# Second products of 512-token slots with the tokens as moving columns, and their results scattered in quarter rows

## Chip, cores and metric

One core of one Trainium2 chip runs the whole kernel as one launch. The metric is device time in microseconds (us), here 2265.47 us, the median of 3 runs (2264.88 to 2266.15). TensorE (PE) multiplies, VectorE (DVE) and ScalarE (ACT) do elementwise work, GpSimd (POOL) issues the indirect DMAs and SyncE (SP) the other DMAs.

## What is computed

An attention with squared ReLU, and on its result a mixture of eight experts, one expert per token (N = 19968 tokens):

```
attn = np.maximum(z @ z.T / S, 0.0) ** 2          # 8 batches, S = 2496
x    = (u * (attn @ v)).reshape(N, 256)
e    = argmax(x @ w_gate)                          # one of 8 experts per token
h    = np.maximum(x[e] @ w1[e], 0.0)               # 256 -> 1024, the first product
y    = h @ w2[e]                                   # 1024 -> 256, the second product
out  = gate_w * sigmoid(x @ w_output_gate)[e] * y
```

Every float32 factor is split into a high and a low part, and a product is three matrix products (low x high, high x low, high x high).

## The kernel before

**Stage one** walks the 8 batches in chunks of up to 512 query tokens (`weigh`, L280). The steps of a `Tail` object, one per call of `advance`, then gate a chunk's result, choose each token's expert and scatter the chunk's token rows into a DRAM table `xs`, sorted by expert (L455: 16 indirect DMAs of 128 pieces for a chunk of 512). A row of `xs` is four segments of 66 words: 64 words of x, then the token's factor and its number.

**Stage two** walks slots of sorted rows. A slot is 512 tokens ("wide", 32 of them) or 256 ("narrow", 18 that always run), all of one expert. `run` takes them one after the other, and while slot i is computed it loads and prepares the next two:

- `load_x` (L655) loads a slot's rows into `sx` with four DMAs of 32 partitions, and the factor and token number of each row into `meta` with a fifth. `load_w` loads the eight weight tiles.
- `turn` (L705) transposes `sx` in 32x32 blocks, so that the features lie on the partitions; `split_x` (L715, L716) and `split_w` (L698 on ACT, L699 on DVE) make high and low parts.
- `up` is the first product: eight banks (one bank is one PSUM tile `sc` of 512 columns; there are three such tiles), each of six matmuls with the weights stationary and 512 tokens moving (L739). After each bank ACT writes the high part `hh` (L748) and DVE the low part `hl` (L749), which frees `sc`.
- `down` is the second product: per 128 tokens 24 matmuls with the hidden values of these tokens stationary and 256 weight columns moving (L767). ACT multiplies by the factor (L775) and POOL scatters 128 rows of 1 KB to `out` (L776).

After each bank of `up` and each quarter of `down` a call of `then` takes one step off the list `later` (the last chunk's `Tail`, the tables of slots) and one off `steps` (parts of the preparation of the next slot). These calls set the written order of the instructions on PE, ACT and DVE, and every engine runs its own list in that order.

`sx`, `hh`, `hl` and stage one's tiles share one pool `act` of 13 tiles of 128 x 1024 words. A new tile waits until everything that reads the one before it in that place is done:

```
y = ys[:, q]
nc.scalar.activation(out=y, in_=yp[:, :D], func=AF.Copy, scale=self.m[:, q, 0:1])
it = nc.gpsimd.indirect_dma_start(
```

Of the kernel before, what the change touches and what calls it, by code (L numbers as in the profile page):

```python
# [7 lines left out]
F32 = mybir.dt.float32  # L8
# [9 lines left out]
P = 128  # L18
# [32 lines left out]
def attention_moe(ctx, tc, zt, zq_in, ut, v, wg, w12, out):  # L51
# [14 lines left out]
    xs_rows = xs.rearrange("(n a) y -> n (a y)", a=4)  # L66

# [547 lines left out]
    def pads():  # L615
# [3 lines left out]
        nc.gpsimd.memset(pad.bitcast(I32)[:, :, SEG - 1 : SEG], NOTOK)  # L619
# [25 lines left out]
    class Slot:  # L645
        def __init__(self, g):
            self.g = g
            self.part = next(p for p in range(3) if g < sum(LENGTHS[: p + 1]))
            self.i = g - sum(LENGTHS[: self.part])
            self.n = TW if self.part < 2 else T  # L650
            self.w = [None] * 8
# [4 lines left out]
        def load_x(self):  # L656
# [4 lines left out]
            self.x = pool.tile([P, 2 * CH], F32, name="sx", tag="act", bufs=13)  # L661
            self.m = pool.tile([P, 4, 2], F32, name="meta", bufs=4)
            its = []
            for a in range(4):
                its.append(
                    nc.sync.dma_start(
                        out=self.x[a * 32 : (a + 1) * 32, 0 : 2 * n].rearrange("r (n y) -> r n y", y=64),
                        in_=rows[:, a * SEG : a * SEG + D // 4].rearrange("(n r) y -> r n y", r=32),
                    )
                )  # L670
            its.append(
                nc.sync.dma_start(
                    out=self.m[:, 0 : n // P], in_=rows[:, SEG - 2 : SEG].rearrange("(q p) d -> p q d", p=P)
                )
            )
# [26 lines left out]
        def turn(self):  # L702
# [4 lines left out]
                in_=self.x[:, 0 : 2 * n].rearrange("p (n k s) -> p k n s", k=2, s=32),  # L707
# [46 lines left out]
        def down(self, then):  # L754
            wb = self.w
            ys = pool.tile([P, 4, D], F32, name="y", tag="xr", bufs=2)
            for q in range(self.n // P):
# [17 lines left out]
                nc.scalar.activation(out=y, in_=yp[:, :D], func=AF.Copy, scale=self.m[:, q, 0:1])  # L775
# [10 lines left out]
                then()  # L786

# [51 lines left out]
    with tc.manual_schedule(engines=all_engines):  # L839
        for k in range(-4, 0):  # L840
            prepare(k, 0 if k < -2 else LEAD)
            if k < -LOOK:
                continue
            make(k + LOOK)
        for k, (b, c, jp) in enumerate(units):
            pos = k % NPAIR
            make(k + LOOK)
            if (b, c, pos) == (B - 1, NCH - 1, 8):
                slots[0].turn()
                slots[0].split_x()  # L850
            if pos == 0:
                o = [ps_o.tile([P, CH], F32, name="o") for _ in range(2)]
                nxt = Tail(b, c, o)
            weigh(b, c, jp, attn.pop(k), o, pos == 0, pos == NPAIR - 1)
            for it in tails:
                it.advance()
            if pos == 6:
                nxt.load()
            if b == B - 1:
                if (c, pos) == (1, 1):  # L860
                    table_steps = full_table(0)
                if (c, pos) >= (1, 1):
                    next(table_steps, None)
                if c == NCH - 1 and pos in (1, 3):
                    slots[0].load_w(range(2 * pos - 2, 2 * pos + 2))
                if c == NCH - 1 and 5 <= pos:
                    slots[1].load_w({5: (0, 1, 2), 6: (3,), 7: (4, 5), 8: (6,), 9: (7,)}[pos])
                if c == NCH - 1 and pos in (5, 9):
                    slots[pos // 9].load_x()
                if c == NCH - 1 and 7 <= pos <= 8:  # L870
                    slots[0].split_w(range(2 * pos - 14, 2 * pos - 12))
# [49 lines left out]
    with tc.manual_schedule(engines=all_engines):  # L921
        run(slots[: NSLOT - N_EXTRA])
# [60 lines left out]
```

## Time and profile before

| | before |
|---|---|
| median of 3 runs | 2265.47 us |
| the profiled execution | 2267.7 us |
| its span (first to last instruction) | 2265.8 us |
| PE busy | 2244.4 us (99%) |
| DVE, ACT, POOL busy | 1744.4, 1472.5, 925.8 us |
| granted TensorE clock | 0.997 of 2.4 GHz |

The profile is of one execution. Its span is 1.9 us less than the execution's own time, which is 2.2 us above the median of the other three runs. Stage one ends at about 1318 us of the span, the wide slots at 2062.5, the narrow ones with the span. Matmuls are pipelined: a matmul's recorded duration is longer than the distance to the next, so a pitch is read from start to start.

### The profile page before, as it was taken

The page shows a single profiled execution, that of the slowest core. Times are in us where ns is not written, and L with a number is a line of the kernel's source. Part 1 is how long each engine was busy: PE and PEld are TensorE (multiplying, and loading weights), DVE is VectorE, ACT ScalarE, POOL GpSimd, SP SyncE. Part 2 cuts the span into 40 slices and gives each one's busy share as a digit, 9 for nine tenths or more (in the row PEclk, how much of TensorE's full clock was granted, in tenths as well). Part 3 has the DMA queues.
Part 4 walks back from the last instruction along what each step waited for, and adds up shares of the span by engine and source line. Part 5 has one row for each costly group of instructions (what it writes and reads, how often), then busy time and mean ns, then how long its engine had stood idle before and what let it go on. Part 6 is the DMA issues. An engine that isn't in the chain of part 4 may idle for free.

```text
span 2265.8 us, 38207 instructions
## 1 busy us (share of the span) xinstructions
PE 2244.4 (99%) x12306; PEld 1965.8 (87%) x12306; DVE 1744.4 (77%) x2840; ACT 1472.5 (65%) x2311; POOL 925.8 (41%) x810
## 2 busy tenths in 40 slices
PE   9999999999999999999999989999999999999998
PEld 7888888888888888888888878999999999999998
DVE  8898889889989889889889767555555555566775
ACT  8767767767677777777677644555555555455665
POOL 0265466566565665565566654111111111111111
PEclk9999999999999999999999999999999999999999
DMA  6794785776866966966956872322331324444431
GB/s 203 185 217 164 203 194 182 211 167 206 216 159 200 223 157 199 232 160 195 230 155 183 188 178 87 96 70 66 81 92 41 92 80 130 141 122 150 117 82 62
DMA packets 406333, 346.41 MB, mean 153 GB/s; under 512 B 141293, under 2 KB 327662, under 8 KB 406128
## 3 DMA queue, kind: packets, MB, share of 16 engines
q1 hardware_dynamic: 378288, 302.34, 50.7%
q0 software_dynamic: 27840, 41.59, 6.0%
q8 instruction: 98, 1.61, 0.3%
q14 instruction: 107, 0.88, 0.1%
HBM read 272.55 MB, written 128.90 MB: 177 GB/s over the span
## 4 chain that ended last, share of the span: by engine, by line
PE 53%; issue 33%; POOL 8%; DVE 2%; DMA 2%; ACT 1%; POOLq 0%; SPq 0%; DVEq 0%; ACTq 0%
PE o L280 43%; POOL out L776 7%; PE sc L206 4%; PE sc L207 4%; PE mp L331 1%; POOL xs L455 1%; DMA z<-td 1%; DVE al L217 1%; DMA sx<-xs 0%; DMA xs<-xr,idx 0%; POOLq L776 0%; DVE t L229 0%; DMA raw<-in_w 0%; DVE t L232 0%; ACT a L208 0%
## 5 line engine op out<-in xcount | busy, mean ns | idle before, releaser
L455 POOL DMA_INDIRECT xs<-xr,idx x624 | 762.3, 1222 | 614.9 <-DVE idx L451 425.6
L280 PE MATMUL o<-ah,v 128*128 128x512 f32 (+1 forms) x3200 | 968.4, 386 | 0.9 <-DVE v L178 0.7
L280 PEld LDWEIGHTS o<-ah,v 128*128 128x128 f32 x3200 | 599.0, 188 | 109.9 <-DVE v L178 2.2
L280 PE MATMUL o<-al,v 128*128 128x512 f32 (+1 forms) x1520 | 586.1, 386 | 0.6 <-DVE al L217 0.4
L767 PE MATMUL o<-w,hh 128*128 128x256 f32 x2624 | 480.4, 283 | 0.0
L776 POOL DMA_INDIRECT out<-y,meta x164 | 160.6, 980 | 717.3 <-ACT y L775 705.9
L699 DVE TENSOR_TENSOR w<-raw,w 128x512 fp32r<-128x512 f32 x400 | 268.8, 684 | 188.8 <-ACT w L698 188.8
L767 PEld LDWEIGHTS o<-w,hh 128*128 128x128 f32 x2624 | 412.7, 192 | 1.3
L739 PE MATMUL sc<-xh,w 128*128 128x512 f32 (+1 forms) x1600 | 378.8, 353 | 7.3 <-ACT xh L715 2.6
L767 PE MATMUL o<-w,hl 128*128 128x256 f32 x1312 | 371.7, 283 | 0.5 <-DVE hl L749 0.5
L208 ACT ACTIVATE a<-sc 128x512 f32<-128x512 f32 (+1 forms) x480 | 251.3, 576 | 178.6 <-PE sc L207 177.8
L217 DVE TENSOR_TENSOR al<-a,ah 128x1024 fp32r<-128x1024 f32 (+1 forms) x232 | 274.2, 1182 | 90.2 <-ACT ah L213 83.3
L280 PEld LDWEIGHTS o<-al,v 128*128 128x128 f32 x1520 | 285.8, 188 | 56.2 <-DVE al L217 3.2
L739 PEld LDWEIGHTS sc<-xh,w 128*128 128x128 f32 x1600 | 271.8, 190 | 47.9 <-DVE hl L749 4.3
L748 ACT ACTIVATE hh<-sc 128x512 fp32r<-128x512 f32 x328 | 196.6, 600 | 129.4 <-PE sc L739 129.2
L775 ACT ACTIVATE y<-o,meta 128x256 f32<-128x256 f32 x164 | 78.0, 475 | 294.5 <-PE o L767 253.9
L767 PEld LDWEIGHTS o<-w,hl 128*128 128x128 f32 x1312 | 251.7, 192 | 2.4 <-DVE hl L749 1.1
L211 ACT ACTIVATE a<-a 128x1024 f32<-128x1024 f32 (+1 forms) x240 | 246.3, 1026 | 7.6
L749 DVE SCALAR_TENSOR_TENSOR hl<-sc,hh 128x512 fp32r<-128x512 f32 x328 | 224.0, 683 | 34.6 <-ACT hh L748 24.3
L698 ACT CAST w<-raw 128x512 fp32r<-128x512 f32 x400 | 239.9, 614 | 0.0
L739 PE MATMUL sc<-xl,w 128*128 128x512 f32 (+1 forms) x800 | 217.0, 353 | 0.5 <-DVE xl L716 0.5
L206 PE MATMUL sc<-z,hl 128*128 128x512 f32 (+1 forms) x480 | 184.0, 383 | 3.0 <-ACT a L208 1.8
(128 smaller groups left out, 2274.4 us busy)
## 6 DMA issues: line engine op xcount, KB each, us to landing
raw<-in_w SPq DMA_DIRECT2D x400, 256.0 KB
td<-t SPq DMA_DIRECT2D x160, 512.0 KB
z<-td SPq DMA_DIRECT2D x640, 128.0 KB
raw<-in_v SPq DMA_DIRECT2D x72, 256.0 KB
u<-in_ut SPq DMA_DIRECT2D x32, 512.0 KB
sx<-xs SPq DMA_DIRECT2D x128, 128.0 KB
raw<-in_zt SPq DMA_DIRECT2D x40, 256.0 KB
raw<-in_zq SPq DMA_DIRECT2D x39, 256.0 KB
```

The lines of the kernel that those rows point to most:

```text
L206: nc.tensor.matmul(out=sc[:, :w], lhsT=st, rhs=ll[:, :w], start=True, stop=False)
L208: nc.scalar.activation(out=a[:, q, :w], in_=sc[:, :w], func=AF.Relu)
L211: nc.scalar.activation(out=a[:, :, :w], in_=a[:, :, :w], func=AF.Square)
L217: nc.vector.tensor_tensor(out=al[:, :, :w], in0=a[:, :, :w], in1=ah[:, :, :w].bitcast(F32), op=ALU.subtract)
L280: nc.tensor.matmul(out=o[d][:, :w], lhsT=vv[:, q, dd], rhs=rhs, start=begins and q == 0 and k == 0, stop=ends and q == 1 and k == len(term ...
L455: it = nc.gpsimd.indirect_dma_start(out=xs[:, :], out_offset=bass.IndirectOffsetOnAxis(ap=idx[:, n : n + 1], axis=0), in_=self.xr[:, n, :] ...
L698: nc.scalar.copy(out=ww[:, 0], in_=wr)
L699: nc.vector.tensor_tensor(out=ww[:, 1], in0=wr, in1=ww[:, 0].bitcast(F32), op=ALU.subtract)
L739: nc.tensor.matmul(out=hp[:, at : at + n], lhsT=wb[2 * d + f // 4][:, ww, fs], rhs=xx[:, d, :], start=k == 0, stop=k == 5,)
L749: nc.vector.scalar_tensor_tensor(out=lo, in0=hp, scalar=0.0, in1=ho.bitcast(F32), op0=ALU.max, op1=ALU.subtract)
L767: nc.tensor.matmul(out=yp[:, :D], lhsT=hx[:, ts], rhs=wb[4 + f // 2][:, ww, ds_], start=k == 0, stop=k == 23,)
L776: it = nc.gpsimd.indirect_dma_start(out=out[:, :], out_offset=bass.IndirectOffsetOnAxis(ap=self.m.bitcast(I32)[:, q, 1:2], axis=0), in_=y, ...
```

## The change

The second product of 29 of the 32 wide slots (all but the first three) swaps its operands: the weights are stationary and 512 tokens move. It makes two halves of 24 matmuls in place of four quarters of 24. Its result has features on the partitions, so DVE transposes each half in 32x32 blocks out of PSUM into `y`, multiplies `y` by the factors, and POOL scatters it in 16 indirect DMAs of 128 quarter rows (256 bytes each) to four places per row of `out`. For this `load_x` reads the whole segment of 66 words, so that factor and token number come with each quarter, and the `meta` DMA falls away for these slots; `turn` also copies the factors (`fac`, ACT) and makes the indices (`to`, DVE). All results `y`, of the other slots too, now come out of the pool `act`. The first entry of `later` is dropped, and both stages stand in one block of fixed order. On the host the columns of w2 are permuted.

```
@@ Slot.__init__
+            self.by_rows = self.n == T or g < 3
@@ load_x
-            self.x = pool.tile([P, 2 * CH], F32, name="sx", tag="act", bufs=13)
-            self.m = pool.tile([P, 4, 2], F32, name="meta", bufs=4)
+            self.x = pool.tile([P, NB, SEG], F32, name="sx", tag="act", bufs=13)
...
-                        in_=rows[:, a * SEG : a * SEG + D // 4].rearrange("(n r) y -> r n y", r=32),
+                        in_=rows[:, a * SEG : (a + 1) * SEG].rearrange("(n r) y -> r n y", r=32),
...
+            if self.by_rows:
+                self.m = pool.tile([P, 4, 2], F32, name="meta", bufs=4)
...
@@ turn
+            if self.by_rows:
+                return
+
+            self.f = pool.tile([P, NB], F32, name="fac", bufs=3)
+            nc.scalar.copy(out=self.f[:, 0 : n // 32], in_=self.x[:, 0 : n // 32, SEG - 2])
+            self.at = pool.tile([P, NB], I32, name="to", bufs=3)
+            nc.vector.scalar_tensor_tensor(
+                out=self.at[:, 0 : n // 32],
+                in0=self.x.bitcast(I32)[:, 0 : n // 32, SEG - 1],
+                scalar=4.0,
+                in1=quarter[:, 0 : n // 32],
+                op0=ALU.mult,
+                op1=ALU.add,
             )
@@ down, now down_rows, and for 29 slots down_columns
-            ys = pool.tile([P, 4, D], F32, name="y", tag="xr", bufs=2)
+            ys = act_f("y").rearrange("p a b -> p (a b)").rearrange("p (q d) -> p q d", d=D)
...
+        def down_columns(self, then):
+            wb, n = self.w, self.n
+            nb = n // 32
+
+            y = act_f("y").rearrange("p a b -> p (a b)").rearrange("p (n y) -> p n y", y=D // 4)[:, 0:nb]
+            for half in range(2):
+                yp = ps_o.tile([P, CH], F32, name="o")
+                k = 0
+                for f in range(8):
+                    bank, at = self.hidden(f)
+                    ds_ = slice((f % 2) * D + half * P, (f % 2) * D + (half + 1) * P)
+                    hh, hl = self.h[bank]
+                    for hx, ww in ((hh, 1), (hl, 0), (hh, 0)):
+                        nc.tensor.matmul(
+                            out=yp[:, 0:n],
+                            lhsT=wb[4 + f // 2][:, ww, ds_],
+                            rhs=hx[:, at : at + n],
+                            start=k == 0,
+                            stop=k == 23,
+                        )
+                        k += 1
+                then()
+                then()
+                nc.vector.transpose(
+                    out=y[:, :, half * 32 : (half + 1) * 32], in_=yp[:, 0:n].rearrange("p (n r) -> p n r", r=32)
+                )
+            nc.vector.tensor_tensor(
+                out=y, in0=y, in1=self.f[:, 0:nb].unsqueeze(2).to_broadcast([P, nb, D // 4]), op=ALU.mult
+            )
+            for q in range(nb):
+                it = nc.gpsimd.indirect_dma_start(
+                    out=out_quarters[:, :],
+                    out_offset=bass.IndirectOffsetOnAxis(ap=self.at[:, q : q + 1], axis=0),
+                    in_=y[:, q, :],
...
@@ after stage one
-    later = [tails[0].advance] + [idle, tail.advance] * TAIL + [idle] * 8 + [pads]
+    later = [idle, tail.advance] * TAIL + [idle] * 8 + [pads]
```

DVE in the middle of the wide slots, before, from the end of one slot's first product to the second bank of the next (`w<-raw` is L699, `hl<-sc,hh` L749, `xl<-xf,xh` L716):

```order
L749 SCALAR_TENSOR_TENSOR hl<-sc,hh 128x512 x2
L716 TENSOR_TENSOR xl<-xf,xh 128x1024
L699 TENSOR_TENSOR w<-raw_15467,w 128x512
L699 TENSOR_TENSOR w<-raw_15503,w 128x512
L699 TENSOR_TENSOR w<-raw_15580,w 128x512
L749 SCALAR_TENSOR_TENSOR hl<-sc,hh 128x512
```

The same stretch of DVE in the changed kernel, where L841 is the transpose of a half, L844 the multiplication by the factors, L704 the weight split and L768 the low part, now with the semaphores that an instruction waits for (DMASW are those of POOL's DMAs):

```order
L768 SCALAR_TENSOR_TENSOR hl<-sc,hh 128x512 [waits Activation_49] x2
L735 TENSOR_TENSOR xl<-xf,xh 128x1024 [waits Activation_49]
L704 TENSOR_TENSOR w<-raw_15467,w 128x512 [waits DMAHW1_49,Activation_49]
L841 STREAM_TRANSPOSE y<-o 128x16x32 [waits PE_49]
L704 TENSOR_TENSOR w<-raw_15503,w 128x512 [waits DMAHW2_49,Activation_49]
L704 TENSOR_TENSOR w<-raw_15580,w 128x512 [waits DMAHW3_49,Activation_49]
L841 STREAM_TRANSPOSE y<-o 128x16x32 [waits PE_49]
L844 TENSOR_TENSOR y<-y,fac 128x1024 [waits DVE_49]
L768 SCALAR_TENSOR_TENSOR hl<-sc,hh 128x512 [waits DMASW4_49,DMASW3_49,DMASW5_49,DMASW2_49,DMASW6_49,DMASW1_49,DMASW7_49,DMASW0_49,Activation_49]
```

The two transposes and the multiplication stand ahead of the next slot's first low part. That low part (the last row) has a new wait for the eight semaphores of POOL's DMAs. In the built program it is for the count of the sixteenth scatter of the wide slot two before, whose `y` had the tile of the pool `act` that this `hl` takes.

PE at the end of a wide slot, before:

```order
L767 MATMUL o<-w,hh 128x256 x2
L767 MATMUL o<-w,hl 128x256
L767 MATMUL o<-w,hh 128x256
L739 MATMUL sc<-xh,w 128x512 x2
L739 MATMUL sc<-xl,w 128x512 x2
```

PE at the same place in the changed kernel (L831 is the second product, L758 the first):

```order
L831 MATMUL o<-hh,w 128x512 x2
L831 MATMUL o<-hl,w 128x512
L831 MATMUL o<-hh,w 128x512
L758 MATMUL sc<-xh,w 128x512 x2
L758 MATMUL sc<-xl,w 128x512 x2
```

Between the first products of two wide slots stand 48 matmuls of 512 columns where 96 of 256 stood.

DVE at the start of slot 0, before (`u<-o,u` is the first step of the last chunk's `Tail`):

```order
L310 SCALAR_TENSOR_TENSOR u<-o,u 128x512 x2
L699 TENSOR_TENSOR w<-raw_15328,w 128x512
L699 TENSOR_TENSOR w<-raw_15390,w 128x512
L749 SCALAR_TENSOR_TENSOR hl<-sc,hh 128x512
L699 TENSOR_TENSOR w<-raw_15330,w 128x512
```

The same place in the changed kernel:

```order
L704 TENSOR_TENSOR w<-raw_15328,w 128x512
L704 TENSOR_TENSOR w<-raw_15390,w 128x512
L768 SCALAR_TENSOR_TENSOR hl<-sc,hh 128x512
L312 SCALAR_TENSOR_TENSOR u<-o,u 128x512 x2
L704 TENSOR_TENSOR w<-raw_15330,w 128x512
```

Each step of the last chunk's `Tail` stands one call of `then` later.

## Rows read from the trace of the kernel before

**Rows 1.** Page, part 1: busy time, share of the span and instructions of each engine.

```profile
PE 2244.4 (99%) x12306; PEld 1965.8 (87%) x12306; DVE 1744.4 (77%) x2840; ACT 1472.5 (65%) x2311; POOL 925.8 (41%) x810
```

**Rows 2.** Windows: one slot: busy us (count) of PE, PEld, DVE, ACT, POOL; PE clock, DMA.

```profile
1512.90:1535.30 22.40, 22.40 (x146) 20.51 (x145) 12.77 (x18) 11.69 (x21) 3.90 (x4) 1.00 0.42 118
```

**Rows 3.** Timeline, PE: start us, us, instruction, around the end of a wide slot.

```profile
1501.40 0.28 PE L767 MATMUL o<-w,hh 128*128 128x256 f32 x1
...
1512.80 0.28 PE L767 MATMUL o<-w,hh 128*128 128x256 f32 x1
1512.91 0.63 PE L739 MATMUL sc<-xh,w 128*128 128x512 f32 x2
...
1523.82 0.28 PE L767 MATMUL o<-w,hh 128*128 128x256 f32 x1
```

**Rows 4.** Timeline, all engines: the hand-overs at the start of that slot.

```profile
1513.12 0.48 ACT L775 ACTIVATE y<-o,meta 128x256 f32<-128x256 f32 x1 [1.90 <-PE o L767]
...
1513.87 0.98 POOL L776 DMA_INDIRECT out<-y,meta  x1 [1.91 <-ACT y L775]
...
1514.50 0.60 ACT L748 ACTIVATE hh<-sc 128x512 fp32r<-128x512 f32 x1 [0.40 <-PE sc L739]
...
1515.13 0.69 DVE L749 SCALAR_TENSOR_TENSOR hl<-sc,hh 128x512 fp32r<-128x512 f32 x1 [0.31 <-ACT hh L748]
```

**Rows 5.** Groups by line, DVE, wide slots (count, busy us, mean ns, idle before).

```profile
L699 DVE TENSOR_TENSOR w<-raw,w 128x512 fp32r<-128x512 f32 x214 | 146.5, 684 | 150.1 <-ACT w L698 150.1
...
L716 DVE TENSOR_TENSOR xl<-xf,xh 128x1024 fp32r<-128x1024 f32 x26 | 31.9, 1226 | 77.8 <-ACT xh L715 77.8
```

**Rows 6.** Line L340: DVE's transpose of 512 columns out of PSUM (ns min/median/max).

```profile
L340 DVE STREAM_TRANSPOSE lt<-mp x40: 586/704/711, 64.8 to 1341.7; 128x512 f32<-128x512 f32 x32, 128x448 f32<-128x448 f32 x8
```

**Rows 7.** Timeline, POOL: the last chunk's 16 scatters, during slots 0 and 1.

```profile
1368.02 0.97 POOL L455 DMA_INDIRECT xs<-xr,idx  x1 [12.12 <-DVE idx L451]
1369.30 0.97 POOL L455 DMA_INDIRECT xs<-xr,idx  x1 [0.30 <-issue]
1370.57 1.93 POOL L455 DMA_INDIRECT xs<-xr,idx  x1 [0.30 <-issue]
1372.81 0.97 POOL L455 DMA_INDIRECT xs<-xr,idx  x1 [0.30 <-issue]
...
1380.48 1.24 POOL L455 DMA_INDIRECT xs<-xr,idx  x1 [0.30 <-issue]
...
1389.94 0.97 POOL L776 DMA_INDIRECT out<-y,meta  x1 [0.30 <-issue]
```

**Rows 8.** Timeline, DVE, beside these scatters.

```profile
1370.43 1.23 DVE L716 TENSOR_TENSOR xl<-xf,xh 128x1024 fp32r<-128x1024 f32 x1 [2.09 <-ACT xh L715]
1372.83 0.71 DVE L699 TENSOR_TENSOR w<-raw,w 128x512 fp32r<-128x512 f32 x1 [1.17 <-ACT w L698]
...
1380.19 0.68 DVE L699 TENSOR_TENSOR w<-raw,w 128x512 fp32r<-128x512 f32 x1
```

**Rows 9.** Groups by line, POOL, whole span.

```profile
L455 POOL DMA_INDIRECT xs<-xr,idx x624 | 762.3, 1222 | 614.9 <-DVE idx L451 425.6 <-issue 173.9 <-DMA sx<-xs 10.2
```

**Rows 10.** Line L455, whole span: time from issue to landing of a scatter.

```profile
L455 POOL DMA_INDIRECT xs<-xr,idx x624: 969/1088/2036, 84.0 to 1388.7; - x156
...
DMA to landing us min/median/max: 2.2/4.4/8.6
```

**Rows 11.** Line L455, 1360 to 1400 us: the same for the last chunk.

```profile
DMA to landing us min/median/max: 2.2/2.2/2.2
```

**Rows 12.** Line L776, wide slots: durations of a scatter of 1 KB rows, and landing.

```profile
L776 POOL DMA_INDIRECT out<-y,meta x107: 972/974/982, 1460.4 to 2049.1; - x107
...
DMA to landing us min/median/max: 2.4/2.4/2.9
```

**Rows 13.** Waits of PE, 1300 to 1450 us: total us, times, longest.

```profile
PE sc L739 <- DVE hl L749: 2.6, 2, 1.6
```

More of the change, by code (lines that the diff above doesn't have):

```diff
@@ L66, in attention_moe @@
     xs_rows = xs.rearrange("(n a) y -> n (a y)", a=4)
+    out_quarters = out.rearrange("n (a y) -> (n a) y", a=4)
     ones = const.tile([P, P], BF16, name="ones")
@@ L754, in down, with down_rows @@
         def down(self, then):
+            if self.by_rows:
+                self.down_rows(then)
+            else:
+                self.down_columns(then)
+        def down_rows(self, then):
             wb = self.w
-            ys = pool.tile([P, 4, D], F32, name="y", tag="xr", bufs=2)
+            ys = act_f("y").rearrange("p a b -> p (a b)").rearrange("p (q d) -> p q d", d=D)
             for q in range(self.n // P):
@@ L838, in attention_moe @@
     all_engines = {mybir.EngineType.PE, mybir.EngineType.Activation, mybir.EngineType.DVE}
[L839 to L871, printed above, removed]
-            if pos == NPAIR - 1:
-                tail = nxt
-                tails = [it for it in tails if it.step < TAIL] + [tail]
-            prepare(k)
@@ new lines, in attention_moe @@
+    ordered = ExitStack()
+    ordered.enter_context(tc.manual_schedule(engines=all_engines))
+    for k in range(-4, 0):
+        prepare(k, 0 if k < -2 else LEAD)
+        if k < -LOOK:
+            continue
+        make(k + LOOK)
+    for k, (b, c, jp) in enumerate(units):
+        pos = k % NPAIR
+        make(k + LOOK)
+        if (b, c, pos) == (B - 1, NCH - 1, 8):
+            slots[0].turn()
+            slots[0].split_x()
+        if pos == 0:
+            o = [ps_o.tile([P, CH], F32, name="o") for _ in range(2)]
+            nxt = Tail(b, c, o)
+        weigh(b, c, jp, attn.pop(k), o, pos == 0, pos == NPAIR - 1)
+        for it in tails:
+            it.advance()
+        if pos == 6:
+            nxt.load()
+        if b == B - 1:
+            if (c, pos) == (1, 1):
+                table_steps = full_table(0)
+            if (c, pos) >= (1, 1):
+                next(table_steps, None)
+            if c == NCH - 1 and pos in (1, 3):
+                slots[0].load_w(range(2 * pos - 2, 2 * pos + 2))
+            if c == NCH - 1 and 5 <= pos:
+                slots[1].load_w({5: (0, 1, 2), 6: (3,), 7: (4, 5), 8: (6,), 9: (7,)}[pos])
+            if c == NCH - 1 and pos in (5, 9):
+                slots[pos // 9].load_x()
+            if c == NCH - 1 and 7 <= pos <= 8:
+                slots[0].split_w(range(2 * pos - 14, 2 * pos - 12))
+        if pos == NPAIR - 1:
+            tail = nxt
+            tails = [it for it in tails if it.step < TAIL] + [tail]
+        prepare(k)
@@ L919, in run @@
             s.down(then)
-    with tc.manual_schedule(engines=all_engines):
-        run(slots[: NSLOT - N_EXTRA])
+    run(slots[: NSLOT - N_EXTRA])
+    ordered.close()
     assert not later
```

31 lines of the change are left out of this document (22 added, 9 removed).

## Prediction

> **What bounds it now.** The page's first part comes first: PE is busy for 99% of the span [rows 1]. That share alone does not say that PE sets the time, so a stage is looked at by itself. In the window of one wide slot PE is busy 22.40 of 22.40 us at full clock (2.4 GHz), DVE 12.77, ACT 11.69 and POOL 3.90 [rows 2]: in the wide slots PE is the bound, and POOL has 18.5 us to spare. How long PE takes is read from start to start [rows 3]. From 1501.40 to 1512.91 lie the 96 matmuls of 256 columns of a second product: 11.51 us, 0.120 each. From 1512.91 to 1523.82 lie the 48 matmuls of 512 columns of the next first product: 10.91 us, 0.227 each. The same columns cost 0.240 us in two matmuls and 0.227 in one, so each matmul carries about 0.013 us that its columns do not explain. A wide slot is 22.42 us.
>
> **PE.** The change puts 48 matmuls of 512 columns where 96 of 256 stood, in 29 slots. At the pitch of the first product that is 48 x 0.227 = 10.91 for 11.51: 0.60 us a slot, 17.4 us in all, if PE stays fed. The wide slot would be 21.82 us.
>
> That is measured in this kernel, on the same engine and type. The Trainium skill (TensorE: Matmul & The Clock Gate, Back-to-back issue gap) gives a fixed 2.5 ns for each matmul behind its columns; by it the 48 fewer would save an estimated 0.12 us a slot, 3.5 us in all. The trace disagrees with it by five times, 13 ns [rows 3].
>
> **ACT and SP.** ACT loses four activations a slot (one is 0.48 us [rows 4]) and gains a copy of 16 words per partition; it was busy half the slot [rows 2], so this is worth nothing. SP loses one of five row loads per slot, and the other four bring 264 bytes for 256 per piece; they are issued two slots ahead of their transpose, which hides them. Both at 0; without that lead a slot would wait for its rows.
>
> **DVE.** Added per slot: two transposes out of PSUM, 0.70 us each [rows 6], a multiplication of 128 x 1024, priced as the subtraction of that size, 1.23 [rows 5], and 0.2 for the indices. DVE rises from 12.8 to about 15.6 us of 21.8. The first transpose lies beside the second half's matmuls. The second and the multiplication lie at the start of the next slot: the last matmul before the slot's end began at 1512.80, ended at 1513.08, and ACT took its result at 1513.12, 0.21 after the next first matmul at 1512.91 [rows 3, 4]. So they run from 0.21 to 0.91 and on to about 2.2 us of the next slot. The first low part started 2.22 us into the slot before [rows 4]: it is not pushed. Cost 0.
>
> **POOL.** Here the change is not hidden. A slot has 16 scatters in place of 4. Free of disturbance one follows the other in 1.28 us, 20.5 us for 16, against a slot of 21.8. But [rows 7] are 16 scatters of nearly this size (66 words a piece for 64), and they take 21.92 us from the first to the start of the next instruction. The third took 1.93 instead of 0.97. [Rows 8] show why: DVE's subtraction of two SBUF operands had begun at 1370.43, before the call at 1370.57, and ended at 1371.66; the call ended 0.84 later. The weight split from 1380.19 to 1380.87 held the call at 1380.48 likewise (1.24). A subtraction that began at 1372.83, just after the call at 1372.81, held nothing. A call that starts while such an instruction runs waits for its end.
>
> The Trainium skill (SBUF — State Buffer, Who interferes with whom) states that a two-input instruction contends with GpSimd's reads, and infers that it leaves descriptor generation alone. By that inference the scatters would not be held and the slot would be PE's 21.82. The held call [rows 7, 8] speaks against the inference: this DMA is held.
>
> **The new wait.** The first low part of a slot waits for the landing of all 16 scatters of the slot two before. Count from E, the end of the slot that made y: multiplication done at E + 2.2; POOL follows its releaser by 0.27 (1513.60 to 1513.87 [rows 4]), so the first call is at E + 2.5; the sixteenth starts 15 x 21.92 / 16 = 20.55 later, at E + 23.0; landing takes 2.2 [rows 11]: E + 25.2. It is due when PE wants the first PSUM tile back for its fourth bank, 3 x 1.364 = 4.09 into the slot, less 0.69 for the low part itself [rows 4]: E + 21.82 + 4.09 - 0.69 = E + 25.2. It just fits, with nothing to spare. Behind the waiting instruction stand all of DVE's weight splits and low parts, and PE waits for the PSUM tile; that a late low part stops PE is seen at the change of stages, 2.6 us in two waits [rows 13].
>
> One more hold tips it. The sixteenth call starts 23.0 - 21.8 = 1.2 us into the next slot, inside the next multiplication (0.91 to 2.2). If it is held as the third call of [rows 7] was, it lands up to 0.96 later, and the next train starts 0.9 later too. PE waits, and since a late PE also moves the next due time, half of it remains: 0.45 a slot. So a wide slot lies between 21.82 (no further hold) and 22.78 (0.96 kept whole). I take 22.2, a little under the half: a held call shifts the following ones, so not every slot meets it.
>
> **Change of stages.** The last chunk's steps stand one call of `then` later. They are the same instructions around the same waits; a late low part there costs up to 1.6 us at a time [rows 13], so the bounds are 1.6 either way, and I take 0.
>
> **Sum.** 29 x (22.42 - 22.2) = 6.4 us less. The profiled execution took 2267.7 us, 1.9 over its span, and would be 2261.3; the median of the runs shown is 2.2 below it, so 2265.5 - 6.4 = 2259.1. A difference under 0.2% (4.5 us) can't be told from none here.
>
> **Rivals.**
> - *No hold on the path.* The multiplication misses the calls, or two-input instructions hardly hold them: the slot is 21.82 to 22.0, 29 x 0.42 to 0.60 = 12 to 17.4 us less, about 2250. Against it: [rows 7, 8]. For it: none of the 107 scatters in the wide slots took over 0.982 us, though each came alone [rows 12]. 0.17. It is what the inference on descriptor generation would give.
> - *The wait gives the gain back.* Holds by both long subtractions in most slots, 22.3 to 22.58: within 4.5 us, 2265. 0.25. By the TensorE page of the Trainium skill, with 3.5 us saved, the time would be about 2262, in this class too, with 0.02 since [rows 3] contradict it. Together 0.27.
> - *Slower: the quarter rows land late.* The place is the same wait. In stage one, with more DMA traffic, the median landing was 4.4 us [rows 10]; 1 KB rows in the wide slots took 2.4 to 2.9 [rows 12]. Each us of landing costs half a us per slot: at 4.4 the slot is 22.2 + 1.1 = 23.3, 25.5 us more, 2291. It decides from 2.2 + 0.44 = 2.64 us on. If instead the calls keep the mean of stage one, 1.22 and 0.31 between [rows 9], POOL is the bound with 16 x 1.53 = 24.5 us: 2325. For both: DVE will be busier. Against: the train of [rows 7] ran in stage two itself. 0.18 together.
> - *The change doesn't do what it says.* PE's written order shows 48 matmuls of 512 columns, so only the pitch could differ; the first product has that shape. Under 0.01.
>
> **Numbers.** My case (22.0 to 22.3) has 0.38, all of it faster by over 0.2%; with the first rival faster is 0.55, same 0.27, slower 0.18. The range reaches to the first rival's 2248 and on the other side to 2272 (22.65), leaving out about 0.15 above and little below.
>
> **What would show it.** PE's second product with a pitch of 0.227; a wide slot of 22.2 us; in it a PE wait at the fourth bank for DVE's low part; the low part waiting for a scatter's landing; POOL busy about 17 us of a slot with one or two calls near 1.9 us. Wrong would be: scatters all of 0.97 us (first rival), landings of over 2.6 us (third), or POOL with no idle time at all.

## The result and the profile after

The changed kernel takes 2286.74 us (median of 6 runs, 2282.94 to 2289.49) against 2265.81 us (6 runs, 2264.88 to 2266.52): a ratio of 1.0091, 95% interval 1.0078 to 1.0104. It is slower by 21 us; the forecast was 2259.1, with a range to 2272. The profiled execution took 2285.96 us, its span is 2284.3.

The page of the changed kernel, first part (answers to [rows 1]), says nothing alarming. PE is still busy for 99%, and POOL has risen from 41% to 57%:

```profile
PE 2251.5 (99%) x10914; PEld 1889.9 (83%) x10914; DVE 1808.4 (79%) x2956; ACT 1422.0 (62%) x2224; POOL 1294.2 (57%) x1158
```

But 1392 fewer matmuls, with the same columns, are busy for 7 us more. The program has stretches whose ends can be compared one by one. The first is stage one, whose instructions the change does not touch. The timeline of PE around its last weighing matmul, before and then after (start us, us, engine, line, operation):

```profile
1317.70 0.62 PE L280 MATMUL o<-ah,v 128*128 128x512 f32 x2
1318.15 0.39 PE L280 MATMUL o<-al,v 128*128 128x512 f32 x1
```

```profile
1329.28 0.62 PE L282 MATMUL o<-ah,v 128*128 128x512 f32 x2
1329.74 0.39 PE L282 MATMUL o<-al,v 128*128 128x512 f32 x1
```

Stage one ends 11.6 us later, though not a step of it was moved. The table takes every stretch from the starts of PE's matmuls (us of the profiled spans); its last column is the version that came out of the experiments:

| stretch | before | after | difference | `e5_y_wide_apart` |
|---|---|---|---|---|
| to the last weighing matmul | 1318.15 | 1329.74 | +11.6 | 1318.26 |
| from there to the first rewritten slot | 81.6 | 78.8 | -2.8 | 79.1 |
| 29 rewritten wide slots | 651.2 | 659.7 | +8.5 | 631.2 |
| narrow slots, to PE's last end | 207.5 | 205.7 | -1.8 | 207.5 |
| from PE's last end to the end | 7.3 | 10.4 | +3.0 | 10.4 |

The rows add up to the 18.4 us by which the spans differ; the medians differ by 21. (The wide slots of the kernel before end at 2051.0 us, the sum of its first three rows; 2062.5 is the end of the first narrow slot.) The growth of the last row is POOL's closing drain, 6.27 us in the trace after and 3.82 before; it is 6.27 in the traces of `e2_act_1088`, `e3_y_apart` and `e5_y_wide_apart` too.

The wide slots were forecast at 22.2 us each and take 22.75 in the mean. Five of the 29 take 24.05 to 26.41, the others 22.1 to 22.8. Two of them, from first matmul to first matmul, one without a stop of PE and the one with the longest (answers to [rows 2]; windows of the changed kernel, busy us and instruction count of each engine):

```profile
core 0: us, PE busy (x) PEld busy (x) DVE busy (x) ACT busy (x) POOL busy (x), PEclk, DMA share, GB/s
1589.01:1611.24 22.23, 22.23 (x98) 18.06 (x97) 14.85 (x22) 9.93 (x18) 14.61 (x15) 1.00 0.51 140
1611.24:1637.65 26.41, 23.98 (x98) 19.11 (x97) 15.05 (x22) 9.93 (x18) 19.00 (x19) 0.94 0.19 46
```

PE is fed without a gap in the first, and it still takes 22.23 where 96 x 0.227 would be 21.8. The second loses 2.4 us of PE's time and has a lower mean clock. Its beginning, DVE first and then PE (timeline of the changed kernel):

```profile
1612.16 1.25 DVE L844 TENSOR_TENSOR y<-y,fac 128x1024 f32<-128x1024 f32 x1
1617.23 0.69 DVE L768 SCALAR_TENSOR_TENSOR hl<-sc,hh 128x512 fp32r<-128x512 f32 x1 [3.83 <-DMA out<-y,to]
...
1614.92 0.62 PE L758 MATMUL sc<-xh,w 128*128 128x512 f32 x2
1617.98 0.99 PE L758 MATMUL sc<-xh,w 128*128 128x512 f32 x2 [2.43 <-DVE hl L768]
1618.77 1.05 PE L758 MATMUL sc<-xl,w 128*128 128x512 f32 x2
```

The first low part waits 3.83 us for the landing of scatters, and PE stops for 2.43 at the fourth bank: the wait of the prediction, at its place. Behind it the next pair starts 0.79 us later instead of 0.46; the granted clock from 1617.70 to 1620.50 is 0.60. The train that this stop waits for (the sixteen scatters of one slot) took 22.99 us, where the others take 20.3 to 21.7. POOL was idle once in it, behind its first call, for 2.13 us in place of 0.30; what held it there the trace doesn't show:

```profile
1591.42 0.97 POOL L848 DMA_INDIRECT out<-y,to  x1 [1.83 <-DVE y L844]
1594.52 0.98 POOL L848 DMA_INDIRECT out<-y,to  x1 [2.13 <-issue]
```

The other four slots of over 24 us have no such pause, and lose about 2 us each. So two things cost time: a wait that was forecast, and a slower pitch that was not.

### The profile page after: what moved, and what is told of

Same layout as the page of the kernel before. It is cut to its first block, busy times and chain, and to the rows that moved or that the text cites. A ratio compares the mean times of both kernels' runs of the same rounds, so it can differ in the third digit from the quotient of the medians.

```text
span 2284.3 us, 36227 instructions
## 1 busy us (share of the span) xinstructions
PE 2251.5 (99%) x10914; PEld 1889.9 (83%) x10914; DVE 1808.4 (79%) x2956; ACT 1422.0 (62%) x2224; POOL 1294.2 (57%) x1158
## 4 chain that ended last, share of the span: by engine, by line
PE 57%; issue 21%; POOL 16%; DMA 2%; DVE 1%; ACT 1%; POOLq 0%; SPq 0%; DVEq 0%; ACTq 0%
PE o L282 44%; POOL out L848 14%; PE sc L208 4%; PE sc L209 4%; POOL out L806 2%; PE mp L333 2%; PE o L792 2%; PE sc L758 1%; DMA out<-y,to 1%; DMA z<-td 1%; DMA raw<-in_w 0%; POOLq L848 0%; DMA sx<-xs 0%; ACT a L210 0%; ACT a L213 0%
## 5 line engine op out<-in xcount | busy, mean ns | idle before, releaser
L457 POOL DMA_INDIRECT xs<-xr,idx x624 | 770.1, 1234 | 619.9 <-DVE idx L453 432.7
L848 POOL DMA_INDIRECT out<-y,to x464 | 473.3, 1020 | 206.8 <-issue 133.8
L758 PE MATMUL sc<-xh,w 128*128 128x512 f32 (+1 forms) x1600 | 387.0, 357 | 16.6 <-DVE hl L768 12.0
L758 PEld LDWEIGHTS sc<-xh,w 128*128 128x128 f32 x1600 | 271.9, 189 | 69.1 <-DVE hl L768 20.1
L831 PE MATMUL o<-hh,w 128*128 128x512 f32 x928 | 293.4, 392 | 0.0
L704 DVE TENSOR_TENSOR w<-raw,w 128x512 fp32r<-128x512 f32 x400 | 264.9, 680 | 27.8 <-ACT w L703 27.8
L768 DVE SCALAR_TENSOR_TENSOR hl<-sc,hh 128x512 fp32r<-128x512 f32 x328 | 223.4, 682 | 54.7 <-DMA out<-y,to 25.9
L703 ACT CAST w<-raw 128x512 fp32r<-128x512 f32 x400 | 234.8, 616 | 0.0
L758 PE MATMUL sc<-xl,w 128*128 128x512 f32 (+1 forms) x800 | 219.5, 355 | 0.0
L831 PEld LDWEIGHTS o<-hh,w 128*128 128x128 f32 x928 | 174.2, 188 | 39.5
L208 PE MATMUL sc<-z,hl 128*128 128x512 f32 (+1 forms) x480 | 185.1, 386 | 2.1 <-ACT a L210 1.8
L209 PE MATMUL sc<-z,hl 128*128 128x512 f32 (+1 forms) x480 | 183.9, 383 | 0.0
L831 PE MATMUL o<-hl,w 128*128 128x512 f32 x464 | 182.0, 392 | 0.0
L841 DVE STREAM_TRANSPOSE y<-o 128x512 f32<-128x512 f32 x58 | 41.6, 717 | 167.6 <-PE o L831 167.6
```

What stands on the lines that cost most here:

```text
L208: nc.tensor.matmul(out=sc[:, :w], lhsT=st, rhs=ll[:, :w], start=True, stop=False)
L209: nc.tensor.matmul(out=sc[:, :w], lhsT=st, rhs=hh[:, :w], start=False, stop=True)
L457: it = nc.gpsimd.indirect_dma_start(out=xs[:, :], out_offset=bass.IndirectOffsetOnAxis(ap=idx[:, n : n + 1], axis=0), in_=self.xr[:, n, :] ...
L703: nc.scalar.copy(out=ww[:, 0], in_=wr)
L704: nc.vector.tensor_tensor(out=ww[:, 1], in0=wr, in1=ww[:, 0].bitcast(F32), op=ALU.subtract)
L758: nc.tensor.matmul(out=hp[:, at : at + n], lhsT=wb[2 * d + f // 4][:, ww, fs], rhs=xx[:, d, :], start=k == 0, stop=k == 5,)
```

## Experiments

All ratios are to the kernel before, run on the same chip. Where nothing else is said that kernel took 2265.8 to 2267.0 us.

**1. What makes every matmul slower.** The change makes a slot's row tile `sx` 4224 bytes long instead of 4096. It shares the rotation `act` with PE's moving tiles, so the thirteen buffers and all behind them moved. First that alone, in the kernel before:

```diff
-self.x = pool.tile([P, 2 * CH], F32, name="sx", tag="act", bufs=13)
+self.x = pool.tile([P, 2 * CH + 32], F32, name="sx", tag="act", bufs=13)
```

> The kernel before with one edit: the buffers of the tag act (moving operands and activations) are 1056 words long instead of 1024, as the change makes them, so that every second of them and all buffers behind them start 128 bytes off their old place within 256 bytes; nothing reads or writes the added words. Theory A (the start address of PE's moving tiles sets the pitch): stage one drifts as in the changed kernel, its last weighing matmul starts at about 1329.7 us in place of 1318.2, the 512-column pitch of stage one is a mean of about 230 ns in place of 227; in a wide slot the 48 matmuls of the first product rise by about 4 ns each, 0.2 us a slot; total about 2283 us, 2277 to 2288. Theory B (the drift comes from the order of the program, the larger DMA pieces or the scatters): 2266 us within 2, and 1318 within 1.

Measured: 2280.32 us, ratio 1.0062 (1.0048 to 1.0076). The last weighing matmul of this run:

```profile
1329.28 0.39 PE L280 MATMUL o<-al,v 128*128 128x512 f32 x1
```

That is 11.1 us late without any of the change's instructions: theory A. Most wide slots are about 22.57 for 22.42, narrow ones 11.41 for 11.52. Next, whether the moving tile's own start decides, or how it stands to the stationary one:

```diff
+const.tile([P, 32], F32, name="gap")    # e6; [P, 16] in e7
 wg_f = const.tile([P, 2, 2 * E], F32, name="wg_f")
```

> The kernel before with all buffers of the pool 128 bytes further, moving and stationary operands alike, by an unused constant of 32 words. Theory A1 (the moving tile's own start decides, 64 of 256 is the dear one): all 512-column matmuls at 231 to 232 ns, stage one's last weighing matmul at about 1340 us, total about 2288 us. Theory A2 (the start of the moving tile against that of the stationary one decides): 227 ns and 2266 us within 2, as before.

> The kernel before with all buffers of the pool 64 bytes further, so that the tiles start at a multiple of 256 bytes. Theory A1 in the form that only 64 of 256 is dear: 227 ns, 2266 us within 2; in the form that only 192 of 256 is cheap: 231 ns or more, 2283 us or more. Theory A2 (the distance between moving and stationary tile decides): 2266 within 2.

Measured: 2267.23 us, 1.0001 (0.9991 to 1.0011), and 2263.19 us, 0.9990 (0.9981 to 1.0000). Neither shift costs anything: what the moving tiles alone did at 128 bytes is gone when the stationary ones go with them. Then the stationary tiles alone, in the rotation `keep`:

```diff
-return lambda tag_name: pool.tile([P, 2, CH], dt, name=tag_name, tag=name, bufs=bufs)
+more = 32 if name == "keep" else 0
+return lambda tag_name: pool.tile([P, 2 * CH + more], dt, name=tag_name, tag=name, bufs=bufs)[
+    :, 0 : 2 * CH
+].rearrange("p (a b) -> p a b", a=2)
```

> The kernel before with buffers of 1056 words in the tag keep (weights of stage two, v and z of stage one) in place of act: every second stationary tile of the weighing starts 128 bytes off, the moving tiles of act stay. Theory A1 (the moving tile decides): of stage one only the 960 matmuls of the scores, half of which move a shifted z, rise: about 2 us, last weighing matmul at 1320; the first products of stage two unchanged; total 2266 to 2270. Theory A2 (distance to the stationary tile, or the stationary tile itself): half of the weighing matmuls at 231 ns or more, 1329 us, total 2280 or more.

Measured: 2281.32 us, 1.0064 (1.0047 to 1.0081):

```profile
1332.59 0.39 PE L283 MATMUL o<-al,v 128*128 128x512 f32 x1
```

14.4 us late, theory A2: the distance decides. With the addresses of the built programs beside the starts in the traces, the weighing matmuls of 512 columns sort like this (mean start to start, ns):

```
distance of the two operands' starts, modulo 256 bytes      0              128
before                                              227.0 (3522)        -
e6, all 128 further                                 227.0 (3524)        -
e7, all 64 further                                  226.8 (3524)        -
e2, act buffers a multiple of 256 again (step 2)    227.0 (3524)        -
e1, every second moving tile 128 off                228.1 (2012)   232.0 (1512)
after                                               228.1 (2012)   232.0 (1512)
e8, every second stationary tile 128 off            227.9 (1706)   232.8 (1818)
```

Within the first column, distances that are 0 and 256 modulo 512 give the same (227.0 both in the kernel before and in e2), so 256 is the period as far as tried; distances other than 0 and 128 did not occur.

**2. The addresses mended, the wait left.** Buffers of 4352 bytes are a multiple of 256 again; three small constants and one small table give the room by sharing the place of other tiles (those lines are left out here):

```diff
-self.x = pool.tile([P, NB, SEG], F32, name="sx", tag="act", bufs=13)
+self.x = pool.tile([P, NB, SEG + 2], F32, name="sx", tag="act", bufs=13)[:, :, 0:SEG]
```

> The changed kernel with buffers of 1088 words in the tag act, a multiple of 256 bytes, so that all moving tiles start where those of the kernel before do within 256 bytes; room for it is made by letting three small constants share the place of later tiles. Theory A (addresses): the last weighing matmul of stage one is back at 1318 us within 1, the 512-column pitch at 227 ns, the wide slot without a wait at 21.8 to 21.95; the waits of PE for low parts stay (about 8 to 14 us in all); total about 2265 us, 2258 to 2270. Theory B (order, DMA or scatters): 2287 us within 3. Theory C (the wait for the scatters is the main cost, addresses nothing): 2287 within 3 too, told from B by the next run.

Measured: 2300.14 us, 1.0148 (1.0133 to 1.0164). A miss for all three theories, and the most telling of the versions. Stage one ends at 1317.48 and a slot without a wait takes 21.76 us, as A said; but PE now stops in every second slot, which takes 26.0. Waits of PE and of DVE for low parts and scatters over the span (us in total, times, longest):

```profile
PE sc L758 <- DVE hl L768: 34.3, 16, 2.9
...
DVE hl L768 <- DMA out<-y,to: 50.5, 14, 4.3
```

One such place, with POOL, DVE and PE (timeline):

```profile
1487.55 0.98 POOL L848 DMA_INDIRECT out<-y,to  x1 [0.30 <-issue]
1488.84 1.97 POOL L848 DMA_INDIRECT out<-y,to  x1 [0.30 <-issue]
...
1488.74 1.22 DVE L844 TENSOR_TENSOR y<-y,fac 128x1024 f32<-128x1024 f32 x1
1493.67 0.69 DVE L768 SCALAR_TENSOR_TENSOR hl<-sc,hh 128x512 fp32r<-128x512 f32 x1 [3.71 <-DMA out<-y,to]
...
1494.41 1.22 PE L758 MATMUL sc<-xh,w 128*128 128x512 f32 x2 [2.38 <-DVE hl L768]
1495.43 1.05 PE L758 MATMUL sc<-xl,w 128*128 128x512 f32 x2
```

The slot whose y this is ended at E = 1466.0. The sixteenth call begins at E + 22.8 (forecast 23.0); the next multiplication, begun 0.10 earlier, holds it to 1.97; it ends at 1490.81, and the low part starts 2.86 later, at E + 27.7. It was due at E + 25.2. So it is 2.5 late: 1.0 by the hold, and 1.6 by a landing of 2.86 us behind the call's end, where 2.2 from its start, 1.2 from its end, had been reckoned. (The trace tells no landing of these scatters by itself; it is read as the start of the low part that waits for it.) In the windows of this place the DMA engines' share is 0.77 at the slot's start, and the clock is halved once PE has stopped:

```profile
1487.79:1491.80 4.01, 4.01 (x19) 3.19 (x17) 1.94 (x2) 2.20 (x4) 3.40 (x3) 1.00 0.77 145
1494.41:1497.00 2.59, 2.59 (x6) 2.10 (x7) 2.59 (x5) 0.00 (x0) 1.98 (x3) 0.50 0.09 29
```

Six matmuls at half the clock (1.2 GHz) add about 1.2 us to the stop of 2.4.

How much of the price is the landing, fourteen such waits of this trace show. In twelve the low part starts 2.7 to 3.4 us behind the call's end, with a DMA share between the two of 0.54 to 0.65. In the last two it starts 1.7 to 1.8 behind it, with a share of 0.28 and 0.29. Two of them, from the call's end to the low part:

```profile
1490.81:1493.67 2.86, 1.22 (x6) 0.68 (x4) 0.00 (x1) 2.11 (x4) 1.95 (x2) 1.00 0.58 100
2016.51:2018.27 1.76, 1.22 (x6) 0.68 (x4) 0.01 (x1) 1.51 (x4) 1.15 (x2) 1.00 0.28 49
```

The sixteenth call is held to 1.98 in the second too, but that slot takes 23.35 us, not 26.0.

**3. The wait taken away.** y of stage two goes back to the two buffers of `xr`, so no low part stands behind scatters; in the changed kernel, then together with the mended addresses:

```diff
-y = act_f("y").rearrange("p a b -> p (a b)")...
+y = pool.tile([P, 2 * CH], F32, name="y", tag="xr", bufs=2)...
```

> The changed kernel with the results y of stage two in the two buffers of the tag xr, as before the change, in place of the rotation of tag act; so no low part stands behind the scatters of an earlier slot. Theory A (addresses cost about 22 us, the wait about 10): PE's waits for low parts fall from 12 us to under 4, the stretch of matmuls at half the clock is gone, stage one still ends at about 1329.7 us; total about 2277 us, 2273 to 2281. Theory C (the wait is the main cost): under 2266. Theory D (POOL's train of 16 scatters is the bound, whatever waits for it): slots stay at 22.3 or above on average and POOL has no idle time between trains; 2283 or more.

> Both edits of the two runs before: buffers of 1088 words and y apart. Theory A: stage one ends at 1318 us, wide slots at 21.8 to 21.95, no wait of PE for low parts in them; total about 2254 us, 2248 to 2259, faster than both kernels. Theory D (POOL's trains pace the slots): slots at 22.0 to 22.4 and about 2262. Theory B: 2277 or more.

Measured: 2276.59 us, 1.0049 (1.0035 to 1.0063), and 2255.97 us, 0.9957 (0.9944 to 0.9971): theory A both times. In `e3_y_apart` the 29 slots take 644.4 us, 22.2 each; in `e4_both` 631.1, 21.76 each, with POOL's trains filling the slot to 0.3 us. Its second and third narrow slots took 16.75 and 13.84 us, ACT waiting for a buffer of y:

```profile
ACT y L800 <- DMA out<-y,to: 8.7, 1, 8.7
```

So y of the slots that scatter whole rows returned to the rotation, one line of `down_rows` against `e4_both`:

```diff
-ys = pool.tile([P, 2 * CH], F32, name="y", tag="xr", bufs=2).rearrange(...)
+ys = act_f("y").rearrange("p a b -> p (a b)").rearrange(...)
```

> The run with both edits, but y of the slots that scatter whole rows (the first three and the narrow ones) back in the rotation of tag act, so that only the quartered slots use the two buffers of xr. In the run with both edits POOL's trains took 21.76 us, as long as the slot, each began 0.3 us behind the last, and the first narrow slots then waited (16.75 and 13.84 us in place of 11.52, PE behind an activation that waited 8.7 us for the landing of the last train). Theory A (that loss is the wait for the buffer alone): the narrow slots are all at 11.5, total 7.5 us less, about 2248.5 us, 2246 to 2251. Theory D (POOL's backlog must be paid before the narrow slots wherever y lies, now by a low part behind the late scatters): some 4 us or more of it remain, 2253 or more.

Measured: 2247.43 us, 0.9911 (0.9894 to 0.9927): theory A, 18 us faster than the kernel before. A wide slot and two narrow ones, PE without a gap:

```profile
1723.90:1745.60 21.70, 21.70 (x97) 17.98 (x96) 15.22 (x22) 9.93 (x18) 16.82 (x17) 1.00 0.23 50
2028.50:2051.50 23.00, 23.00 (x193) 22.99 (x192) 17.27 (x27) 13.71 (x26) 17.81 (x18) 1.00 0.47 133
```

**4. What holds a call.** In the kernel of step 2 two instructions with one SBUF tile replace the multiplication. They leave out the row's own factor, so the results are not those of the task, and only the times count:

```diff
-nc.vector.tensor_tensor(out=y, in0=y, in1=self.f[...]..., op=ALU.mult)
+for _ in range(2):
+    nc.vector.tensor_scalar(out=y, in0=y, scalar1=self.f[:, 0:1], scalar2=None, op0=ALU.mult)
```

> The run with buffers of 1088 words (y in the rotation, 2300 us) with the multiplication of y, which reads two SBUF operands, replaced by two instructions that read one SBUF tile and scale it by the first of the factors, so that DVE is busy with y about as long; y is scaled by one factor per partition in place of one per row. Theory H (a scatter's call is held only by an instruction with two SBUF operands; the hold by the multiplication tips the wait): no call is held beside the two, trains of 16 take 20.5 to 21.4 us, the slots stay at 21.8 to 22.0, PE's waits for low parts fall under 5 us from 34, total 2248 to 2256. Theory L (any long DVE instruction on SBUF holds a call, or the wait comes from the landing alone): trains of 22.3 us in every second slot as before, 2290 us or more.

> The changed kernel with buffers of 1088 words once more, as the comparison for the next run on the same chip. On a chip where the kernel before takes 2266 us it should take 2300 us, with trains of 22.3 us in every second slot.

> The kernel with the two one-input instructions in place of the multiplication once more, since on the first chip the activations of the slots started 3 to 4 us after their data at places where the kernel before lost 15 us too, so that the run of that call measured something else. Theory H (only an instruction with two SBUF operands holds a scatter's call): trains of 20.5 to 21.4 us, slots of 21.8 to 22.0, total 2248 to 2256 us. Theory L (any long DVE instruction on SBUF holds it, or the landing decides): 2290 us or more, trains of 22 us. Theory M (the replacement itself is slow, on any chip): activations late by 3 to 4 us again and 2500 us, while the run beside it takes 2300.

> The kernel with two one-input instructions in place of the multiplication of y, once more, for a chip on which the kernel before takes 2266 us; on the two chips so far it took 2281 and 2284 and activations began late there. On a chip of 2266: Theory H (only an instruction with two SBUF operands holds a scatter's call, and the hold by the multiplication tips the wait) trains of 20.5 to 21.4 us, slots of 21.8 to 22.0, PE's waits for low parts under 5 us, total 2248 to 2256 us. Theory L (any long DVE instruction on SBUF holds the call, or the landing decides) trains of 22 us or more in every second slot and 2290 us or more. On a chip of 2281 or more: 2500 us again, and nothing is told.

> The kernel with two one-input instructions in place of the multiplication of y, a last time, for a chip on which the kernel before takes 2266 us. Theory H (only an instruction with two SBUF operands holds a scatter's call): trains of 20.5 to 21.4 us, slots of 21.8 to 22.0, PE's waits for low parts under 5 us, total 2248 to 2256 us. Theory L (any long DVE instruction on SBUF holds the call, or the landing decides): trains of 22 us or more in every second slot, 2290 us or more. On another chip it tells nothing.

The first three times it ran on other chips (step 6): 2535.72, 2610.19 and 2535.68 us, and 2630.14 for the kernel of step 2; they decide nothing here. The fourth time it was on a chip where the kernel before took 2267.02: 2280.97 us (2263.20 to 2287.16), 1.0047 (1.0022 to 1.0071), between the theories. The calls of the 464 scatters of quarter rows, sorted by what DVE ran when each began (trace):

```
DVE at the call's start                        e2: calls, held, mean us    e17: calls, held, mean us
nothing                                          182    0   0.97             170    0   0.97
low part (one operand in PSUM)                   142    0   0.97             162    0   0.97
transpose of rows, indices                        28    0   0.97              26    0   0.97
weight split, two SBUF operands                   70   66   1.22              65   56   1.14
xl split, two SBUF operands                       28   27   1.35              27   26   1.40
multiplication of y, two SBUF operands            14   14   1.98               -
scaling of y, one SBUF tile                        -                          14    0   0.97
```

A held call ends 0.85 us behind the instruction. Calls beside two SBUF operands that were not held had begun in the last 0.15 us of the instruction, where the call's own 0.97 us reach as far, or within 0.03 us of its start, as the three beside the multiplication in the changed kernel. So that half of theory H, that nothing else holds a call, is right without an exception. Its other half is not: the trains fell from 22.33 to 21.0 us, but PE still waits,

```profile
PE sc L758 <- DVE hl L768: 25.3, 18, 2.4
```

since in the stopped slots the low part starts about 3.3 us behind the last call's end, and the longer scaling of y starts the train later. The 29 slots take 667.1 us, against 685.7 with the hold and 631.1 without the wait (step 3). So the hold is a part of the price, here about 19 of 55 us, and the late landing the larger one, as the two short waits of step 2 also say.

**5. The order alone.** The kernel before with one manual schedule over both stages (not shown) and the shortened list:

```diff
-later = [tails[0].advance] + [idle, tail.advance] * TAIL + [idle] * 8 + [pads]
+later = [idle, tail.advance] * TAIL + [idle] * 8 + [pads]
```

> The kernel before with the order part of the change alone: one manual schedule over both stages, and the list of later steps without the early call for the last tail. Theory (the change of stages gains by the order, since the first slots' steps no longer stand beside that early step): from the last weighing matmul (1318.2 us) to the first slot that the change rewrites it takes 78.8 us in place of 81.6, total about 2263 us. Rival (the gain comes from y and the rows of the first slots lying elsewhere): 81.6 us as before, 2266 us within 2.

> The kernel before with the order part of the change alone, once more, for a chip on which the kernel before takes 2266 us. Theory (the order gives the 2.9 us at the change of stages): 78.8 us from the last weighing matmul to the first slot that the change rewrites, 2263 us. Rival (y and the first slots' rows in other buffers give it): 81.6 us or more, 2266 us or more.

Measured: 2281.04 us for 2280.91, 1.0003 (0.9993 to 1.0012), and 2280.58 for 2280.29, 1.0004 (0.9993 to 1.0014), both on chips of step 6. A gain of 2.8 us (0.9988) is excluded there. On the other chips the 2.8 us are within what this stretch varies by: `e7_all_64` takes 76.6 us for it and `e6_all_128` 83.3, with the order of the kernel before (81.6), and the versions with the new order take 78.1 to 80.2. One trace of each can't tell the order's share.

**6. Other chips.** On three of the chips the kernel before takes 2280 to 2284 us.

> The best version so far (buffers of 1088 words, y of the quartered slots apart) once more beside the other two. On a chip where the kernel before takes 2266 us: 2247 us. On a chip where it takes 2281 us or more, where activations began late beside POOL's trains: slower than the kernel before if that lateness belongs to the trains (over 2400 us), about 2262 if it belongs to the wait for the scatters.

> The changed kernel itself once more, beside the run before. On a chip where the kernel before takes 2266 us: 2287 us. On a chip where it takes 2280 us or more: if POOL's trains are what makes the activations late there, well over 2400 us, since every one of the 29 slots has a train as long as itself; if the chip is slow in another way, some 15 us over 2287.

Measured: 2510.29 us, 1.0996 (1.0971 to 1.1022), for the version that gains 18 us elsewhere; the changed kernel itself ran on a chip of 2267.02 and repeated its result, 2285.33, 1.0077 (1.0057 to 1.0097). In a wide slot of `e15_best_again`, ACT and then PE (timeline):

```profile
1711.28 0.60 ACT L767 ACTIVATE hh<-sc 128x512 fp32r<-128x512 f32 x1 [2.56 <-PE sc L758]
1716.95 0.60 ACT L767 ACTIVATE hh<-sc 128x512 fp32r<-128x512 f32 x1 [4.56 <-remote]
1721.85 0.60 ACT L767 ACTIVATE hh<-sc 128x512 fp32r<-128x512 f32 x1 [4.31 <-remote]
...
1711.44 0.61 PE L758 MATMUL sc<-xh,w 128*128 128x512 f32 x2
1717.60 0.50 PE L831 MATMUL o<-hh,w 128*128 128x512 f32 x1 [1.47 <-issue]
1722.50 0.80 PE L831 MATMUL o<-hh,w 128*128 128x512 f32 x1 [3.45 <-issue]
```

PE's last bank is done at 1712, but the activations of the last two begin at 1716.95 and 1721.85, with ACT idle, while POOL's train runs (1703.46 to 1723.58). Their only waits in the program are for PE. `e14_order_again` has the same beside the one train of its wide slots, in a slot of 36.8 us for 22.4; that may be the 15 us by which these chips are slower before the change, though the kernel before was not traced there. Why a handover is late on them stays open; the changed kernel itself was not run on one.

## Why the prediction was wrong

Of the 18.4 us by which the spans differ, the addresses cost about 23 (11.6, 13 and -1.8), the new wait 15 and the drain 3; the wider matmuls give back 20 and the change of stages 2.8.

- **PE's pitch: right as a rate, and it is what a slot gets.** With the operands at one distance the slot is 21.76 us, forecast 21.82; 29 slots give back 20 us. The page TensorE: Matmul & The Clock Gate of the Trainium skill (Back-to-back issue gap) would have given an estimated 0.12 us a slot; the runs measure 0.66 (22.42 less 21.76).
- **"ACT and SP ... Both at 0": the step that failed first.** The wider row pieces were priced as a transfer. Their tile is the largest of the rotation that also holds PE's moving operands, so 66 words for 64 moved every one of them, and all buffers behind. It costs 11.6 us in stage one, which the prediction did not even list as touched, and 0.46 a slot (22.22 in `e3_y_apart` for 21.76), 13 us; the narrow slots return 1.8.
- **The new wait: place and chain right, two sizes wrong.** The sixteenth call began at E + 22.8 for 23.0. Landing was reckoned as 2.2 us from the call's start, 1.2 from its end, from the change of stages [rows 11]; the low parts that waited for it started 2.1 to 3.6 us behind the call's end in the changed kernel (14 waits) and 1.7 to 3.4 in `e2_act_1088` (14). The DMA engines are busy for 0.77 at that moment, a slot's start, and the two waits of `e2_act_1088` beside a DMA share of 0.3 were the short ones; that the traffic is why was not tried by itself. And after a stop of 2.4 us six matmuls ran at half the clock, which the term did not have. With fed slots it costs 1.9 us each (685.7 us for 29 in `e2_act_1088`, 631.1 without it), not 0.4. In the changed kernel it costs 15 us (659.7 against 644.4), 0.5 a slot, and that this is near 0.4 is luck: the further hold that the term was made of never came, since the sixteenth call took 0.97 us in 28 of its 29 trains (1.17 in the last). That it costs less there than in `e2_act_1088` fits a slot that is 0.46 us longer and leaves POOL as much more.
- **The hold of calls: right.** Two SBUF operands hold, others do not, 0.85 us past the instruction's end. A train of the changed kernel takes 20.3 to 21.7 us, and 22.99 in the one with the pause (forecast 21.92, which counts the step to the next instruction); no call there takes over 1.67. The Trainium skill's inference (SBUF — State Buffer, Who interferes with whom) that such an instruction leaves descriptor generation alone can't be carried over to these scatters: 107 calls are held in `e2_act_1088`. A call here also reads its indices (`to`) from SBUF; whether that reading or the descriptors are what is held, no run here tells.
- **Change of stages and end.** -2.8 us, outside the bounds of 1.6; kernels with one and the same order differ by up to 6.7 us in this stretch (step 5), so the bounds were too narrow and no cause is shown. +3.0 us for POOL's drain, which had no term.
- **The rivals.** "The quarter rows land late" is what happened at the wait; it was given 0.18. That its 2291 us lies near the 2286.74 measured is luck: the wait made 15 us of the loss, and the addresses, which were no rival at all, 23. Without the rise of the pitch the total would have been that of `e2_act_1088`, slower still.

## What to carry to other kernels

When a tile in a shared rotation changes its size, look at the addresses of everything behind it: with buffers that are a multiple of 256 bytes, moving and stationary tiles kept the same place within 256, and PE its pitch. A stage that the change does not touch is the best control: compare its end first. Before a buffer is shared with a queue that lands late, count from the landing beside the traffic of that very moment; a buffer of its own took 53 us off here (`e2_act_1088` to `e5_y_wide_apart`).

## What the runs showed that was not expected

- 512-column matmuls (fp32r) start 227 ns apart where the starts of both operands are equal modulo 256 bytes, and 232 to 233 apart at a distance of 128. With equal starts the place itself changed nothing (0, 64 and 192 were tried). Narrow slots, of 256 columns and with mixed distances, were a little quicker: 11.41 us for 11.52.
- Mending one of two costs made the kernel slower: 2300 us for 2287, as a faster PE ran into a wait that the slower one had mostly missed.
- On three chips every version with trains in the wide slots took 2510 to 2630 us. In the trace of the best one activations begin 2 to 5 us late while a train runs; the cause is open.
